# Gated linear attention and a GELU feed-forward: two stages with a DRAM bridge, rewritten as one software pipeline over 512-token groups

## The chip, the cores and the metric

The kernel runs on one core of a Trainium2 chip. The metric is the device time of one execution in microseconds (us). A core has a matrix engine (PE, whose weight loads are listed apart as PEld), a vector engine (DVE), an activation engine (ACT), a general engine (POOL) and SP, which here issues DMAs.

## The reference

```python
f = 1.0 / (1.0 + np.exp(-f_logit))
state = np.zeros((B, H, D, D), dtype=np.float32)
for t in range(S):
    state = f[:, :, t, :, None] * state + np.einsum('bhd,bhe->bhde', k[:, :, t], v[:, :, t])
    y[:, :, t] = np.einsum('bhd,bhde->bhe', q[:, :, t], state)
x = np.ascontiguousarray(y.transpose(0, 2, 1, 3)).reshape(B * S, H * D)
h = x @ w_in
out = (0.5 * h * (1.0 + erf(h / sqrt(2)))) @ w_out
```

B is 4, H is 8, S is 768, D is 48: 3072 tokens of 384 features. The hidden width d_ff is 2048. Inputs and output are float32.

## The kernel before

The recurrence is computed in chunks of 128 tokens, nC = 6 chunks for each of the 32 pairs (b, h). The decay becomes a running sum of log f, taken with a triangular matrix on PE (line 80), so that Q is scaled by exp of the sum and K by its reciprocal (lines 84 to 92). Per chunk, PE transposes both to 48x128 (lines 101, 103), makes the 128x128 scores AT (line 109), which ACT copies and POOL masks (lines 110, 111), and the chunk's contribution to the 48x48 state (line 116), which DVE scales and accumulates (lines 117 to 128). Two matmuls then make the output, transposed, in YT (lines 134, 135). DVE copies it and SP stores it to a DRAM tensor, `xT_bridge` (lines 137, 138).

When the attention pools are closed, the second stage loads the weights through SP, casts them on DVE (lines 150 to 156), and takes 512 tokens at a time: three matmuls into a bank `hps` for each of 16 slices of d_ff (line 172), a gelu on ACT (line 175), and four matmuls into four banks `opsum` (line 177), which DVE copies out and SP stores (lines 181, 182). There are four hps banks and four opsum banks.

The Tile framework orders the instructions of each engine by its own scheduler: it moves pieces of neighbouring (b, h) past each other. Each engine takes its own in order, and waits on semaphores. SP's queue holds the loads, the bridge's 192 stores, and only then the two weight loads and the loads of line 167.

Of the kernel before, what the change touches and what calls it, by code (L numbers as in the profile page):

```python
# [8 lines left out]
F32 = mybir.dt.float32  # L9
AF = mybir.ActivationFunctionType  # L10
ALU = mybir.AluOpType


@with_exitstack
def kernel(
# [10 lines left out]
    nc = tc.nc  # L26
    B, H, S, D = q.shape
    C = 128
    nC = S // C
    d_model = moe_w_in.shape[0]  # L30
    d_ff = moe_w_in.shape[1]
    n_tok = B * S
    assert d_model == H * D

    BF16 = mybir.dt.bfloat16
    xT = nc.dram_tensor("xT_bridge", (d_model, n_tok), BF16, kind="Internal").ap()

    singles = ctx.enter_context(tc.tile_pool(name="singles", bufs=1))
    tri = singles.tile([C, C], BF16)
    nc.gpsimd.memset(tri, 0.0)  # L40
    nc.gpsimd.affine_select(
        out=tri, in_=tri, compare_op=ALU.is_gt, fill=1.0,
        base=0, pattern=[[-1, C]], channel_multiplier=1,
    )
    ident = singles.tile([C, C], BF16)
    make_identity(nc, ident)
    ones_col = singles.tile([C, 1], BF16)
    nc.gpsimd.memset(ones_col, 1.0)

    attn_ctx = ExitStack()  # L50
    sb = attn_ctx.enter_context(tc.tile_pool(name="sb", bufs=4))
    ps = attn_ctx.enter_context(tc.tile_pool(name="ps", bufs=1, space=bass.MemoryType.PSUM))
    s0_pool = attn_ctx.enter_context(tc.tile_pool(name="s0", bufs=4))

    q_r = q.rearrange("b h (c t) d -> b h t c d", t=C)
    k_r = k.rearrange("b h (c t) d -> b h t c d", t=C)
    v_r = v.rearrange("b h (c t) d -> b h t c d", t=C)
    f_r = f_logit.rearrange("b h (c t) d -> b h t c d", t=C)

    for b in range(B):  # L60
        for h in range(H):
            fl = sb.tile([C, nC, D], F32)
            nc.sync.dma_start(out=fl, in_=f_r[b, h])
            q_td = sb.tile([C, nC, D], F32)
            nc.sync.dma_start(out=q_td, in_=q_r[b, h])
            k_td = sb.tile([C, nC, D], F32)
            nc.sync.dma_start(out=k_td, in_=k_r[b, h])
            vv_f = sb.tile([C, nC, D], F32)
            nc.sync.dma_start(out=vv_f, in_=v_r[b, h])
            vv_all = sb.tile([C, nC, D], BF16)  # L70
            nc.vector.tensor_copy(vv_all, vv_f)

            sig = sb.tile([C, nC, D], F32)
            nc.scalar.activation(sig, fl, AF.Sigmoid)  # L74
            lf = sb.tile([C, nC, D], BF16)
            nc.scalar.activation(lf, sig, AF.Ln)  # L76

            gln = ps.tile([C, nC, D], F32)
            glast_p = ps.tile([D, nC], F32)
            nc.tensor.matmul(gln.rearrange("c n d -> c (n d)"), tri, lf.rearrange("c n d -> c (n d)"), start=True, stop=True)  # L80
# [38 lines left out]
            S_all = sb.tile([D, nC, D], BF16)  # L119
# [93 lines left out]
```

## Time and profile before

| | |
|---|---|
| runs | 514.59, 513.13, 513.49 us; median 513.49 |
| profiled execution | span 513.5 us, first to last instruction; 7385 instructions |
| PE busy | 371.6 us, 72% |
| ACT busy | 342.9 us, 67% |
| DVE busy | 256.6 us, 50% |
| POOL busy | 65.0 us, 13% |
| granted clock of PE, mean | 0.994 of full speed |
| DMA | 35.10 MB, 68 GB/s over the span |

The profile lists how long each engine was at work, what each group of instructions cost (line, tile written and tile read, shapes, count, busy time, mean), and what ended the idle time before it (the releaser). The chain of waits follows the last instruction back from releaser to releaser. A queue is written SPq. A busy PE is not a full PE, since ends of pipelined matmuls are modelled.

### The profile page before, as it was taken

How to read it: one execution, taken by the hardware profiler on the slowest of the kernel's cores; microseconds unless marked ns; L12 is line 12 of the kernel's file. 1: busy time of each engine (PE TensorE's matmuls, PEld its weight loads, DVE VectorE, ACT ScalarE, POOL GpSimd, SP SyncE). 2: the span in 40 equal slices, each digit the busy share in tenths (PEclk: the TensorE clock that was granted, in tenths of full speed). 3: DMA queues.
4: the chain of work that ended last, by engine and by line, in shares of the span. 5: the costliest groups of instructions: out<-in, count | busy, mean ns of one | idle time of the engine just before them, and what ended most of it. 6: DMA issues, size and time to landing. Idle time of an engine off the chain costs nothing.

```text
span 513.5 us, 7385 instructions
## 1 busy us (share of the span) xinstructions
PE 371.6 (72%) x2048; PEld 183.1 (36%) x2048; DVE 256.6 (50%) x1018; ACT 342.9 (67%) x897; POOL 65.0 (13%) x201
## 2 busy tenths in 40 slices
PE   1666666655677776677877777674179899999995
PEld 0333333332333343343434443332034344444442
DVE  1777767776667567755567777863220110101001
ACT  8999999999998889978785454432034344444442
POOL 0021121111111211222221121211000000000000
PEclk9999999999999999999999999999989999999998
DMA  9544433334334224322322220002910211201011
GB/s 164 83 97 98 97 63 79 64 63 94 66 66 86 53 45 93 68 43 43 73 42 57 45 56 11 7 9 54 396 49 0 93 57 37 92 2 63 0 63 61
DMA packets 121002, 35.10 MB, mean 68 GB/s; under 512 B 113152, under 2 KB 120576, under 8 KB 120576
## 3 DMA queue, kind: packets, MB, share of 16 engines
q1 hardware_dynamic: 120960, 34.63, 29.4%
q8 instruction: 16, 0.26, 0.2%
q14 instruction: 26, 0.21, 0.1%
HBM read 27.53 MB, written 7.08 MB: 67 GB/s over the span
## 4 chain that ended last, share of the span: by engine, by line
PE 46%; ACT 34%; issue 8%; DMA 6%; DVE 6%; POOL 0%; SPq 0%; ACTq 0%; DVEq 0%
PE opsum L177 13%; PE hps L172 11%; PE AT L109 6%; ACT L76 5%; ACT L74 5%; PE YT L135 5%; ACT KpT L106 4%; ACT ATm_all L110 4%; PE KpTp L103 4%; DMA wout_f<-in_moe_w_out_dram 4%; ACT L84 4%; PE YT L134 3%; ACT QpT_all L104 3%; PE QpTp L101 2%; ACT lf L76 2%
## 5 line engine op out<-in xcount | busy, mean ns | idle before, releaser
L175 ACT ACTIVATE gT<-hps 128x512 bf16<-128x512 f32 x96 | 57.2, 597 | 77.2 <-PE hps L172 61.0
L111 POOL TENSOR_SCALAR_AFFINE_SELECT ATm_all<-ATm_all 128x128 bf16<-128x128 bf16 x192 | 63.9, 333 | 286.2 <-ACT ATm_all L110 286.1
L137 DVE CAST YTs<-YT 48x128 bf16<-48x128 f32 x192 | 52.4, 273 | 70.2 <-PE YT L135 68.5
L109 PE MATMUL AT<-QpT_all,KpT 48*128 48x128 bf16 x192 | 54.7, 285 | 45.0 <-ACT KpT L106 44.0
L172 PE MATMUL hps<-xTt,win_sb 128*128 128x512 bf16 x288 | 73.3, 387 | 16.0 <-DVE win_sb L152 16.0
L177 PE MATMUL opsum<-wout_sb,gT 128*128 128x384 bf16 x384 | 75.0, 333 | 5.0 <-DVE wout_sb L156 2.8
L181 DVE COPY osb<-opsum 128x384 f32<-128x384 f32 x24 | 12.3, 552 | 119.2 <-PE opsum L177 109.2
L134 PE MATMUL YT<-ATm_all,vv_all 128*48 128x128 bf16 x192 | 58.4, 304 | 18.0 <-DVE YTs L137 15.1
L110 ACT ACTIVATE ATm_all<-AT 128x128 bf16<-128x128 f32 x192 | 51.8, 270 | 27.9 <-PE AT L109 27.9
L104 ACT ACTIVATE QpT_all<-QpTp 48x128 bf16<-48x128 bf16 x192 | 50.2, 261 | 20.9 <-PE QpTp L101 19.4
L117 DVE TENSOR_SCALAR Scon_all<-Scontrib,Glast_all 48x48 f32<-48x48 f32 x192 | 48.6, 253 | 30.2 <-PE Scontrib L116 26.5
L88 DVE RECIPROCAL rGT_all<-GT_all 128x288 f32<-128x288 f32 x32 | 61.9, 1935 | 1.5 <-ACT GT_all L84 1.5
L101 PE MATMUL QpTp<-ident,Qp_all 128*48 128x128 bf16 x192 | 58.1, 303 | 5.4 <-ACT QpT_all L104 3.2
L116 PE MATMUL Scontrib<-vv_all,Kp_all 128*48 128x48 bf16 x192 | 44.0, 229 | 20.7 <-DVE Scon_all L117 18.2
L103 PE MATMUL KpTp<-ident,Kp_all 128*48 128x128 bf16 x192 | 57.8, 301 | 0.1
L135 PE MATMUL YT<-QpT_all,S_all 48*48 48x128 bf16 x192 | 57.4, 299 | 0.0
L106 ACT ACTIVATE KpT<-KpTp 48x128 bf16<-48x128 bf16 x192 | 50.8, 264 | 4.7 <-PE KpTp L103 3.0
L109 PEld LDWEIGHTS <-KpT 48*128 48x128 bf16 x192 | 19.4, 101 | 88.8 <-ACT KpT L106 78.6
L177 PEld LDWEIGHTS <-gT 128*128 128x128 bf16 x384 | 31.3, 99 | 47.8 <-ACT gT L175 27.4
L172 PEld LDWEIGHTS <-win_sb 128*128 128x128 bf16 x288 | 28.5, 99 | 46.1 <-issue 19.3
L76 ACT ACT_TABLE_LOAD x32 | 41.1, 1283 | 0.9 <-PE glast_p L82 0.3
L74 ACT ACT_TABLE_LOAD x29 | 37.2, 1283 | 1.3 <-PEq L197 0.8
(37 smaller groups left out, 389.2 us busy)
## 6 DMA issues: line engine op xcount, KB each, us to landing
fl<-in_f_logit_dram SPq DMA_DIRECT2D x32, 144.0 KB, 2.7
q_td<-in_q_dram SPq DMA_DIRECT2D x32, 144.0 KB, 2.6
k_td<-in_k_dram SPq DMA_DIRECT2D x32, 144.0 KB, 2.6
vv_f<-in_v_dram SPq DMA_DIRECT2D x32, 144.0 KB, 2.5
out_dram<-osb SPq DMA_DIRECT2D x24, 192.0 KB, 2.0
xT_bridge<-YTs SPq DMA_DIRECT2D x192, 12.0 KB, 1.4
win_f<-in_moe_w_in_dram SPq DMA_DIRECT2D x1, 3072.0 KB, 10.0
wout_f<-in_moe_w_out_dram SPq DMA_DIRECT2D x1, 3072.0 KB, 19.2
```

What stands on the lines that cost most here:

```text
L76: nc.scalar.activation(lf, sig, AF.Ln)
L101: nc.tensor.transpose(QpTp, Qp, ident)
L103: nc.tensor.transpose(KpTp, Kp, ident)
L104: nc.scalar.activation(QpT_all[:, c, :], QpTp, AF.Copy)
L106: nc.scalar.activation(KpT, KpTp, AF.Copy)
L109: nc.tensor.matmul(AT, KpT, QpT_all[:, c, :], start=True, stop=True)
L110: nc.scalar.activation(ATm_all[:, c, :], AT, AF.Copy)
L111: nc.gpsimd.affine_select(out=ATm_all[:, c, :], in_=ATm_all[:, c, :], compare_op=ALU.is_ge, fill=0.0, base=0, pattern=[[1, C]], channel_mu ...
L134: nc.tensor.matmul(YT, vv_all[:, c, :], ATm_all[:, c, :], start=True, stop=False)
L135: nc.tensor.matmul(YT, S_all[:, c, :], QpT_all[:, c, :], start=False, stop=True)
L172: nc.tensor.matmul(hps, win_sb[:, ko, fo * 128:(fo + 1) * 128], xTt[:, ko, :], start=(ko == 0), stop=(ko == KO - 1))
L177: nc.tensor.matmul(opsum[s], gT[:, s * 128:(s + 1) * 128], wout_sb[:, fo, :], start=(fo == 0), stop=(fo == FO - 1))
```

## The change

The loops over (b, h) and the second stage go. The 24 chunks of 128 tokens, all eight heads each, are taken in six groups of four: 512 tokens, one tile of the feed-forward part.

- **Stage 1 of a group** (`stage1`): exp(-f_logit) in place, then Ln(x + 1), which is -log f; the running sum with a negated triangular matrix `trin`; gt and rg are Exp of the sum and of its negative; DVE multiplies q and k by them, POOL casts v into `vp`, a padded layout. Sixteen matmuls and an Exp give the decay over each chunk, gl.
- **Attention of a chunk** (`attn`): two heads are put side by side on the partitions (48 of 64 each). Eight transposes fill one bank `tp`; ACT copies kT, DVE makes qb (two copies into a block layout with zeros), ACT copies qT. Scores come in two halves through one bank `ap`, masked by DVE. The state is updated with DVE (the sum) and POOL (the product and the casts into `sb`). The output goes through bank `yp` straight to xT in SBUF, in a row order that w_in's rows are loaded in as well.
- **Feed-forward of a group** (`ffn_group`): f1 is 16 units of three matmuls and a gelu; f2 is, for each of four blocks of 128 tokens, four units of four matmuls into one bank `op`, which ACT copies to `osb`.
- **Order**: the schedule is the order of the code (`manual_schedule`). In round g, f1 and f2 of group g are laid between the attention units of group g+1 and the stage 1 units of group g+2.
- **Loads**: inputs are loaded by SP per chunk and tensor, 16 DMAs a group. The weights are loaded and cast to bfloat16 by 28 DMAs on POOL's queue, at the start.

The diff, cut to its core:

```diff
-    for b in range(B):
-        for h in range(H):
...
-                nc.sync.dma_start(out=xT[h * D:(h + 1) * D, b * S + t0: b * S + t0 + C], in_=YTs)
-    attn_ctx.close()
...
+    ctx.enter_context(tc.manual_schedule())
+    ld = ctx.enter_context(tc.tile_pool(name="ld", bufs=2))
+    hp = ctx.enter_context(tc.tile_pool(name="hp", bufs=3, space=PSUM))
+    pp = ctx.enter_context(tc.tile_pool(name="pp", bufs=1, space=PSUM))
...
+    def load_win():
+        for kk in range(KO):
+            for g in range(4):
+                for hh in range(2):
+                    r = (2 * kk + hh) * D + 16 * g if g < 3 else (6 + hh) * D + 16 * kk
+                    nc.gpsimd.dma_start(out=win[32 * g + 16 * hh:32 * g + 16 * hh + 16, kk, :],
+                                        in_=moe_w_in[r:r + 16, :])
...
+        def u_exp(j):
+            nc.scalar.activation(t["fl"][:, j], t["fl"][:, j], AF.Exp, scale=-1.0)
+        def u_ln(j):
+            nc.scalar.activation(lf[:, j, :, 0:D], t["fl"][:, j], AF.Ln, bias=1.0)
+        def u_g(j):
+            gps = hp.tile([C, H, D], F32, name="hps")
+            nc.tensor.matmul(gps, trin, lf[:, j, :, 0:D], start=True, stop=True)
+            nc.scalar.activation(gt, gps, AF.Exp)
+            nc.scalar.activation(rg, gps, AF.Exp, scale=-1.0)
+            nc.vector.tensor_tensor(qp[:, j, :, 0:D], t["qt"][:, j], gt, ALU.mult)
+            nc.vector.tensor_tensor(kp[:, j, :, 0:D], t["kt"][:, j], rg, ALU.mult)
...
+        def u_t():
+            tp = pp.tile([C, 2, P2, C], BF16, name="tp")
+            for i, src in enumerate((kp, qp)):
+                for p in range(P2):
+                    nc.tensor.transpose(tp[:, i, p, :], src[:, j, 2 * p:2 * p + 2, :], ident)
+            nc.scalar.activation(kT, tp[:, 0], AF.Copy)
+            nc.vector.tensor_copy(qb[0:D, :, 0, :], tp[0:D, 1])
+            nc.vector.tensor_copy(qb[64:64 + D, :, 1, :], tp[64:64 + D, 1])
+            nc.scalar.activation(qT, tp[:, 1], AF.Copy)
+        def u_a(half):
+            ap_ = pp.tile([C, 4, C], F32, name="ap")
+            for i in range(2):
+                p = 2 * half + i
+                nc.tensor.matmul(ap_[:, 2 * i:2 * i + 2, :], x["kT"][:, p, :], x["qb"][:, p],
+                                 start=True, stop=True)
+            nc.vector.tensor_tensor(x["am"][:, 4 * half:4 * half + 4, :], ap_,
+                                    mask.unsqueeze(1).to_broadcast([C, 4, C]), ALU.mult)
...
+        def f1(fo):
+            hps = hp.tile([C, TOK], F32, name="hps")
+            for kk in range(KO):
+                nc.tensor.matmul(hps, win[:, kk, fo * 128:(fo + 1) * 128], xT[:, kk, :],
+                                 start=(kk == 0), stop=(kk == KO - 1))
+            nc.scalar.activation(gT[:, fo, :], hps, AF.Gelu)
+        def f2(s, r):
+            if r == 0:
+                st["o"] = pp.tile([C, d_model], F32, name="op")
+            for fo in range(4 * r, 4 * r + 4):
+                nc.tensor.matmul(st["o"], gT[:, fo, s * C:(s + 1) * C], wout[:, fo, :],
+                                 start=(fo == 0), stop=(fo == FO - 1))
+            if r == 3:
+                nc.scalar.activation(osb, st["o"], AF.Copy)
+                nc.sync.dma_start(out=out[r0:r0 + C, :], in_=osb)
...
+    load(0)
+    load_win()
+    load(1)
+    load_wout()
+    for f in stage1(0):
+        f()
+    spread(attn_group(0), stage1(1), 0.3, 1.0)
+    for g in range(NG):
+        f1, f2 = ffn_group(g)
+        if g + 2 < NG:
+            load(g + 2)
+        att = attn_group(g + 1) if g + 1 < NG else []
+        st1 = stage1(g + 2) if g + 2 < NG else []
+        k1 = len(att) // 2
+        spread(f1, att[:k1])
...
+        spread(f2, seq, 0.0, 0.85)
```

How this moves instructions is seen on three engines. On ACT, before, in the attention stage: copies of one chunk, and table loads between them.

```order
L106 ACTIVATE KpT<-KpTp 48x128
L104 ACTIVATE QpT_all<-QpTp 48x128
L86 ACTIVATE Glast_all<-glast_p 48x6
L74 ACT_TABLE_LOAD
L74 ACTIVATE sig<-fl 128x288
L110 ACTIVATE ATm_all<-AT 128x128
L106 ACTIVATE KpT<-KpTp 48x128
L104 ACTIVATE QpT_all<-QpTp 48x128
L76 ACT_TABLE_LOAD
L76 ACTIVATE lf<-sig 128x288
```

Now, in a steady round (the kernel's lines are those of the new file: 282 gelu, 190 and 195 the copies kT and qT, 130 exp, 133 Ln, 294 osb):

```order
L282 ACTIVATE gT<-hps 128x512 x7
L190 ACTIVATE kT<-tp 128x512
L195 ACTIVATE qT<-tp 128x512
L282 ACTIVATE gT<-hps 128x512 x8
L190 ACTIVATE kT<-tp 128x512
L195 ACTIVATE qT<-tp 128x512
L130 ACT_TABLE_LOAD
L130 ACTIVATE fl<-fl 128x384 x3
L294 ACTIVATE osb<-op 128x384
L130 ACTIVATE fl<-fl 128x384
L133 ACT_TABLE_LOAD
L133 ACTIVATE lf_96<-fl 128x8x48
```

Gelus of one group and attention copies of the next now stand in one row, and the copy of an output block, osb, stands behind a table load and three exps.

On PE, before, in the attention stage: short matmuls of neighbouring chunks.

```order
L116 MATMUL Scontrib<-vv_all,Kp_all 48x48
L109 LDWEIGHTS KpT
L109 MATMUL AT<-QpT_all,KpT 128x128
L103 LDWEIGHTS Kp_all
L103 MATMUL KpTp<-ident,Kp_all 48x128
L134 LDWEIGHTS vv_all
L134 MATMUL YT<-ATm_all,vv_all 48x128
L101 LDWEIGHTS Qp_all
L101 MATMUL QpTp<-ident,Qp_all 48x128
```

Now, in the first half of a round (280 is hps, 202 the scores):

```order
L280 LDWEIGHTS win
L280 MATMUL hps<-xT,win 128x512
L280 LDWEIGHTS win
L280 MATMUL hps<-xT,win 128x512
L280 LDWEIGHTS win
L280 MATMUL hps<-xT,win 128x512
L202 LDWEIGHTS kT
L202 MATMUL ap<-qb_103,kT 128x256
L202 LDWEIGHTS kT
L202 MATMUL ap<-qb_103,kT 128x256
L280 LDWEIGHTS win
L280 MATMUL hps<-xT,win 128x512
```

Feed-forward matmuls now stand between the links of the attention chain.

On POOL, before, from its first instructions (names of the masks and of ATm_all as in the code):

```order
L40 MEMSET tri 128x128
masks.py:197 MEMSET ident 128x128
L41 ISA
L41 AFFINE_SELECT tri<-tri 128x128
masks.py:199 AFFINE_SELECT ident<-ident 128x128
L48 MEMSET ones_col 128x1
L111 AFFINE_SELECT ATm_all<-ATm_all 128x128 x192
```

Now, at the same place (104 and 110 are the weights, 148 the cast of v, 224 and 229 the state):

```order
L90 MEMSET kp_100 128x32x16
L104 DMA win<-in_moe_w_in_dram 16x2048 x24
L110 DMA wout<-in_moe_w_out_dram 128x4x384 x4
L148 CAST vp_101<-vt 128x8x3x16 x4
L229 CAST sb_106<-tn 48x4x3x16 x2
L224 TENSOR_TENSOR tn<-rr,gl 128x384
L229 CAST sb_105<-tn 48x4x3x16 x2
L224 TENSOR_TENSOR tn<-rr,gl 128x384
```

The weights' 28 DMAs have moved from SP, where they came after all of attention, to POOL, ahead of the first cast of v.

## Rows read from the trace of the kernel before

**Rows 1.** The page's part 1: busy time and share of the span, each engine.
```profile
PE 371.6 (72%) x2048; PEld 183.1 (36%) x2048; DVE 256.6 (50%) x1018; ACT 342.9 (67%) x897; POOL 65.0 (13%) x201
```

**Rows 2.** Windows by stage: stretch, its length, busy time by engine, PE's granted clock, DMA share, GB/s.
```profile
12.80:345.00 332.20, 230.43 (x1329) 119.06 (x1330) 229.46 (x958) 270.11 (x772) 62.13 (x186) 1.00 0.31 62
...
355.00:372.00 17.00, 1.95 (x5) 0.73 (x6) 3.36 (x1) 0.44 (x1) 0.00 (x0) 1.00 0.89 328
372.00:513.50 141.50, 131.06 (x668) 59.12 (x666) 15.62 (x25) 58.05 (x97) 0.00 (x0) 0.98 0.14 48
```

**Rows 3.** The page's part 4: the chain that ended last, by engine.
```profile
PE 46%; ACT 34%; issue 8%; DMA 6%; DVE 6%; POOL 0%; SPq 0%; ACTq 0%; DVEq 0%
```

**Rows 4.** The page's part 6, DMA issues: count, KB each, us to landing.
```profile
xT_bridge<-YTs SPq DMA_DIRECT2D x192, 12.0 KB, 1.4
...
wout_f<-in_moe_w_out_dram SPq DMA_DIRECT2D x1, 3072.0 KB, 19.2
```

**Rows 5.** Timeline of SP: start us, us, queue, line; the first loads and the last stores.
```profile
8.43 0.70 SPq L69 DMA_DIRECT2D vv_f<-in_v_dram  x1
...
336.13 18.61 SPq L138 DMA_DIRECT2D xT_bridge<-YTs  x14
```

**Rows 6.** Groups on ACT: line, tile, shapes, count, busy us, mean ns, idle before, releasers.
```profile
L175 ACT ACTIVATE gT<-hps 128x512 bf16<-128x512 f32 x96 | 57.2, 597 | 77.2 <-PE hps L172 61.0 <-PE opsum L177 13.9
...
L110 ACT ACTIVATE ATm_all<-AT 128x128 bf16<-128x128 f32 x192 | 51.8, 270 | 27.9 <-PE AT L109 27.9
...
L76 ACT ACT_TABLE_LOAD x32 | 41.1, 1283 | 0.9 <-PE glast_p L82 0.3
...
L76 ACT ACTIVATE lf<-sig 128x288 bf16<-128x288 f32 x32 | 14.2, 442 | 0.4
```

**Rows 7.** Chain of waits in the feed-forward stage: start us, us, what.
```profile
450.23 1.36 PE opsum L177 x8
451.59 1.29 PE hps L172 x6
```

**Rows 8.** Groups on the weight loads of PE, on DVE and on POOL.
```profile
L111 POOL TENSOR_SCALAR_AFFINE_SELECT ATm_all<-ATm_all 128x128 bf16<-128x128 bf16 x192 | 63.9, 333 | 286.2 <-ACT ATm_all L110 286.1
...
L137 DVE CAST YTs<-YT 48x128 bf16<-48x128 f32 x192 | 52.4, 273 | 70.2 <-PE YT L135 68.5
...
L177 PEld LDWEIGHTS <-gT 128*128 128x128 bf16 x384 | 31.3, 99 | 47.8 <-ACT gT L175 27.4 <-issue 6.5
...
L90 DVE TENSOR_TENSOR Qp_all<-q_td,GT_all 128x288 bf16<-128x288 f32 x32 | 14.2, 443 | 1.7 <-PE QpTp L101 1.7
...
L181 DVE COPY osb<-opsum 128x384 f32<-128x384 f32 x24 | 12.3, 552 | 119.2 <-PE opsum L177 109.2 <-DMA out_dram<-osb 10.0
```

**Rows 9.** Timeline of PE: the first decay sums, and the first feed-forward matmuls.
```profile
6.19 0.40 PE L82 MATMUL glast_p<-ones_col,lf 128*48 128x1 bf16 x6
...
370.43 6.18 PE L172 MATMUL hps<-xTt,win_sb 128*128 128x512 bf16 x20
```

**Rows 10.** Timeline of ACT around a table load, and of two neighbouring evacuations.
```profile
7.59 1.28 ACT L76 ACT_TABLE_LOAD   x1
8.88 0.44 ACT L76 ACTIVATE lf<-sig 128x288 bf16<-128x288 f32 x1
...
16.61 0.26 ACT L110 ACTIVATE ATm_all<-AT 128x128 bf16<-128x128 f32 x1
16.77 0.26 ACT L104 ACTIVATE QpT_all<-QpTp 48x128 bf16<-48x128 bf16 x1
```

**Rows 11.** Windows of 3 us: the first input loads, and the weight loads.
```profile
6.00:9.00 3.00, 0.59 (x7) 0.42 (x7) 0.31 (x1) 2.96 (x4) 0.00 (x0) 1.00 1.35 194
...
364.00:367.00 3.00, 0.00 (x0) 0.00 (x0) 0.41 (x1) 0.00 (x0) 0.00 (x0) 1.00 1.00 399
```

**Rows 12.** The end of the chain of waits.
```profile
506.61 1.00 PE opsum L177 x5
...
508.22 1.90 DMA out_dram<-osb
```

More of the change, by code (lines that the diff above doesn't have):

```diff
@@ L9, with spread @@
 F32 = mybir.dt.float32
+BF16 = mybir.dt.bfloat16
 AF = mybir.ActivationFunctionType
 ALU = mybir.AluOpType
+def spread(main, fill, lo=0.0, hi=1.0):
+    n, m, done = len(main), len(fill), 0
+    for i, f in enumerate(main):
+        f()
+        share = ((i + 1) / n - lo) / (hi - lo)
+        want = min(m, max(0, int(share * m + 0.5)))
+        while done < want:
+            fill[done]()
+            done += 1
+    while done < m:
+        fill[done]()
+        done += 1
 @with_exitstack
@@ L29 @@
     nC = S // C
+    NCH = B * nC
     d_model = moe_w_in.shape[0]
     d_ff = moe_w_in.shape[1]
[L32 to L44, printed above, removed]
@@ new lines @@
+    nc.gpsimd.memset(mask, 0.0)
+    nc.gpsimd.affine_select(out=mask, in_=mask, compare_op=ALU.is_gt, fill=1.0,
+                            base=0, pattern=[[-1, C]], channel_multiplier=1)
+    negcol = one.tile([C, 1], BF16, name="negcol")
+    nc.gpsimd.memset(negcol, -1.0)
+    lfs = [one.tile([C, GC, H, 64], BF16, name=f"lf{i}") for i in range(2)]
+    qps = [one.tile([C, GC, H, 64], BF16, name=f"qp{i}") for i in range(2)]
+    kps = [one.tile([C, GC, H, 64], BF16, name=f"kp{i}") for i in range(2)]
@@ new lines, with load_wout @@
+    win = one.tile([C, KO, d_ff], BF16, name="win")
+    wout = one.tile([C, FO, d_model], BF16, name="wout")
+    def load_win():
[5 more added lines that the diff above has]
+                                        in_=moe_w_in[r:r + 16, :])
+    def load_wout():
+        wo = moe_w_out.rearrange("(fo fi) m -> fi fo m", fi=128)
+        for j in range(4):
+            nc.gpsimd.dma_start(out=wout[:, 4 * j:4 * j + 4, :], in_=wo[:, 4 * j:4 * j + 4, :])
@@ new lines, in attn_group @@
+    def attn_group(g):
+        G[g]["xT"] = ffn.tile([C, KO, TOK], BF16, name="xT")
+        us = [attn(g * GC + j) for j in range(GC)]
+        seq = []
+        for j in range(GC):
+            a = us[j]
+            seq += [a[0], a[1], a[2], a[3], a[4]]
+        order = []
+        for j in range(GC):
+            a = us[j]
+            if j == 0:
+                order.append(a[0])
+            order += [a[1], a[3], a[2]]
+            if j + 1 < GC:
+                order.append(us[j + 1][0])
+            order.append(a[4])
+        return order
@@ new lines @@
+    load(0)
[3 more added lines that the diff above has]
+    for f in stage1(0):
+        f()
+    spread(attn_group(0), stage1(1), 0.3, 1.0)
[7 more added lines that the diff above has]
+        spread(f1, att[:k1])
+        a2, seq = att[k1:], []
+        n = max(len(a2), len(st1))
+        for i in range(n):
+            seq += st1[i:i + 1] + a2[i:i + 1]
+        spread(f2, seq, 0.0, 0.85)
```

249 lines of the change are left out of this document (130 added, 119 removed).

## The prediction

> **What bounds the kernel now.** I read the page's totals first: no engine is full, PE at 72% and ACT at 67% [rows 1]. Such an average hides the stages, so next come the windows by stage [rows 2]. They show three stretches that share almost nothing. Up to 345 us attention runs with ACT busy 270 of 332 us and PE 230, much of it waiting on short results. From 355 to 372 us nearly everything stands while weights arrive at 328 GB/s. From 372 us the feed-forward part runs: PE busy 131 of 141.5 us, ACT 58. The chain of waits over the span agrees: PE 46%, ACT 34%, DMA 6% [rows 3]. So ACT's and PE's idle halves lie at different times, and laying them on each other is where time can come from. The profiled execution's span is 513.5 us; the median of the runs is 513.49, so the sum below needs no correction.
>
> **What goes.** The 192 bridge stores, each 1.4 us to landing [rows 4], and the 17 us gap go; SP's queue ran 18.6 us for the last 14 stores [rows 5], and the weights stood behind them. Sigmoid and reciprocal go. Table loads of 1283 ns fall from 32 in one row alone [rows 6] to 22 in all, counted in the new ACT order. Per (batch, head) 128x48 pieces become four paired heads at a time: each ACT or DVE instruction covers 384 or 512 columns in place of 128, so its fixed part is paid less often.
>
> **PE per group of 512 tokens.** In the feed-forward stage the chain advances 6 hps matmuls in 1.29 us (0.215 each) and 8 opsum in 1.36 us (0.170) [rows 7]: 48 x 0.215 + 64 x 0.170 = 10.3 + 10.9 us. For 128-column attention matmuls, which each bring new weights, no row repeats the form. Below: opsum's rate per column, 0.170 x 128/384 = 0.057 us. Above: the weight load of 99 ns if nothing hides it [rows 8]. Six one-column matmuls with 48-column weights took 0.40 us [rows 9], so neither end is reached there; I take the middle, 0.08. Per chunk: 8 transposes 0.64, 4 score matmuls of 256 columns at 0.107 = 0.43, 4 state 0.32, 12 output 0.96: 2.35 us. Four chunks 9.4, four decay sums 0.7, 16 end sums 1.3. PE needs 10.3 + 10.9 + 11.4 = **32.6 us per group**. The Trainium skill, TensorE: Matmul & The Clock Gate, section Back-to-back issue gap, gives 81 ns for such a stream of weight load and matmul; by it the sum would stand, and no row here shows it.
>
> **ACT per group.** A 512-column evacuation takes 597 ns and one of 128 takes 270 ns [rows 6], so 0.85 ns a column; 384 columns from PSUM take 0.49 us, from SBUF 442 + 96 x 0.85 = 0.52. Sixteen gelus 9.6; eight copies kT, qT 4.8; exp and ln 8 x 0.52 = 4.2; gt, rg 8 x 0.49 = 3.9; four osb 2.0; gl 0.2; four table loads (Exp, Ln, Exp, Gelu) 5.1. In the new order qT also waits for DVE's two qb copies, which wait for kT; DVE's PSUM reads took 273 ns at 128 columns and 552 at 384 [rows 8], so 1.09 ns a column and 0.69 us for 512: four waits of 1.4 us, 5.6. That is 35.4 us without overlap. Two evacuations started 0.16 us apart though each took 0.26 [rows 10], so some 15 neighbours give back 0.1 each: **34 us**. Behind a waiting qT stand the gelus, and behind them PE, which has three hps banks.
> A table load ended at 8.87 us and the next activation began at 8.88 [rows 10], so I charge 1.283 us and no more. The Trainium skill, ScalarE: Activation LUTs, section What ACT_TABLE_LOAD costs, adds a drain of about 1.38 us for each switch: 22 x 1.38 = 30 us more in the sum, were it so; this trace shows none.
>
> **Others.** DVE per chunk: two 384-column products 0.55 each (443 ns at 288 columns [rows 8]), qb 1.4, two masks 1.4, state 0.55, four xT copies 0.55 + 3 x 0.27: 5.8 us, 23 per group, beside the 37.5 below. POOL: one 384-column product and three casts; affine_select took 333 ns for 128 columns [rows 8], so at most three times that each, 4 us per chunk, 16 per group, hidden. Loads: 3.15 MB per group at the 194 GB/s of the first loads [rows 11] is 16 us of each group; SP issues them ahead of the next outputs, each issue about 0.7 us [rows 5]. They cost nothing while a group lasts over 25 us.
>
> **Handoffs.** With PE at 32.6 and ACT at 34, neither can run free. There is one bank for op: s1 cannot start until osb of s0 is copied, and that copy stands on ACT behind kT, qT, a table load and three exps (0.6 + 1.4 + 0.6 + 1.3 + 1.6 = 5.5 us after f2 starts), while PE reaches it after about 4 (16 opsum 2.7, one output 0.96, half a score, one state). PE loses some 1.5 us there, 1 at s2, whose bank waits for the Ln load, kT and qT ahead of osb of s1, and 0.9 when the Gelu table loads after osb of s3; in f1 the wait for qb and for gelu costs about 1.5. PE 32.6 + 4.9 = **37.5 us per group**, between 34 (ACT's sum, all else hidden) and 42 (half of ACT's overlap lost and each handoff 1 us later).
>
> **Start.** ACT's first four exps come before any Ln, so the 13th of 16 loads gates them: 2.56 MB at 194 GB/s is 13 us plus 2.5 to the first data. The weights (6.3 MB, 16 us at the 399 GB/s of the old weight loads [rows 11]) now go at the same time through POOL's queue with a cast, and POOL casts vp, which the first state matmul needs, only after all 28 of them. POOL's issue price has no row. Below, 28 x 0.7 as on SP's queue [rows 5] put the first vp cast at 22 us; above, it stands behind all 12.6 MB, 16 + 33 us, at 52; I take 36, about the middle, for the first state matmul. The 13th load I put at 20 us and the end of the first stage 1 at 29 (9.3 us of ACT), between 16 without weights and 32 with all ahead. Alone, a chunk costs DVE's 4.7 us (without the products): 45.5 after two. Group 1's last fl is the 29th load, 5.7 MB; alone 32 us, with all weights ahead 48; I take 42. Then exp, Ln table, three ln, kT, qb, qT, ln, Exp table: 50, and the last chunk's 7.7 us on DVE with the products: 58. PE then meets a dense stream after sparse work; after the pause at 355 us the first 20 hps took 6.18 us [rows 9] where 20 x 0.215 is 4.3, so I add 2: **60 us** (50 to 75).
>
> **Sum.** Start 60; groups 0 to 3, 4 x 37.5 = 150; group 4 without stage 1: PE 30.7 + 3.3 = 34; group 5 alone: 10.3 + 10.9 + three osb handoffs of 0.8 + 0.4 = 24; tail 0.49 + 0.5 + 1.9 for the last store [rows 12] = 3. **271 us.** Ends: 50 + 4 x 34 + 31 + 23 + 3 = 243 and 75 + 4 x 42 + 38 + 26 + 3 = 310.
>
> **Rivals.** (a) *The stages do not overlap.* Every order is fixed; if each handoff is late, a group costs its feed-forward (22.9 us, a sixth of 370.4 to 507.6 [rows 9, 12]) plus its attention alone (4 x 5.8 on DVE, 12.2 of stage 1 on ACT): 58. Then 60 + 4 x 58 + 46 + 24 + 3 = 365. For it: one bank each for tp, ap, sp, yp, op, and ap is used twice per chunk. Against: two to four feed-forward units stand between links of the attention chain. 0.10.
> (b) *Handoffs hide.* ACT at 34 is the period: 243 if the start is 50 too. For it: before, PE was busy 131 of 141.5 us beside ACT with four banks [rows 2]. Against: one op bank. 0.13.
> (c) *Weights hold up the inputs.* Loads come in 192-byte pieces, weights in long ones. If weights win every turn and the cast runs at a third of the 399 GB/s, they take 48 us, the 29 loads 30 us more, and 16 + 2 follow the 29th as above: start 96, sum 307. Its chance is 0.12: the only rows with heavy traffic have one busy queue, so they speak neither way. The Trainium skill, DMA: Bandwidth & Descriptors, section Queues, rings and completion order, says that an engine takes turns between its queues packet by packet, so that long packets would get more than short ones; no run here shows it.
> (d) *Slower than before.* The cast loads trickle: 28 DMAs, eight outstanding, POOL blocked, group 0's state and all of f1 behind them. From 271 to 515 needs the start at 304 us, 10.8 us for each of the 28 one after another; the bridge's stores ran 1.33 us each so [rows 5], and a whole weight of 3 MB took 19.2 us [rows 4]. 0.03, with 0.01 for about equal.
> (e) That the change doesn't interleave is excluded by PE's order, which shows hps matmuls between score matmuls.
>
> **Numbers.** Forecast 0.61, (a) 0.10, (b) 0.13, (c) 0.12, (d) 0.04 with its neighbour. The range 243 to 315 takes the forecast's ends, most of (b) and the near part of (c); 0.18 stays out. A measurement tells 0.3%, 1.5 us, from no change: faster 0.96, same 0.01, slower 0.03.
>
> **What would show it.** Right: the first hps matmul at 50 to 70 us; six rising blocks some 37 us apart; ACT busiest, near 85%, with 22 table loads; osb the releaser of PE at s1; qT waiting for DVE. Wrong: a first hps after 80 us, with POOL's queue the releaser (c, d); groups of 55 us or more with DVE or POOL naming PE's waits (a); 34 us or less (b). The forecast fails if the group period leaves 34 to 42 us or the start 50 to 75.

## Result and profile after

The changed kernel takes **263.77 us** (median of 4 runs, 262.81 to 265.64) against 513.31 us (median of 4) for the kernel before on the same chip: ratio 0.5147, 95% interval 0.5124 to 0.5169. The forecast was 271, its range 243 to 315. The profiled execution is the slowest of the four, 265.64 us; its span, first to last instruction, is 263.9.

The page of the profiled execution after: totals, slices of 6.6 us each, the costliest groups, and the DMA issues.

```profile
span 263.9 us, 3983 instructions
...
PE 188.5 (71%) x1432; PEld 116.3 (44%) x1432; DVE 129.9 (49%) x266; ACT 160.8 (61%) x292; POOL 61.7 (23%) x125
...
PE   0001364525997887996879968879788799789984
...
ACT  2005832673677867878778787588886785209611
...
PEclk9999999975799999999999979999999999999999
DMA  8999999999400117991149920099910000010011
...
L290 PE MATMUL op<-wout,gT 128*128 128x384 bf16 x384 | 74.4, 330 | 15.1 <-ACT osb L294 15.1
L280 PE MATMUL hps<-xT,win 128*128 128x512 bf16 x288 | 72.2, 387 | 1.0 <-DVE xT L248 0.9
L282 ACT ACTIVATE gT<-hps 128x512 bf16<-128x512 f32 x96 | 54.5, 599 | 7.0 <-PE hps L280 5.0
...
L192 DVE COPY qb<-tp 48x512 bf16<-48x512 bf16 x24 | 10.0, 417 | 43.9 <-ACT kT L190 43.8
L195 ACT ACTIVATE qT<-tp 128x512 bf16<-128x512 bf16 x24 | 14.3, 598 | 23.6 <-DVE qb L193 23.6
L130 ACT ACTIVATE fl<-fl 128x384 f32<-128x384 f32 x24 | 11.6, 516 | 27.1 <-DMA fl<-in_f_logit_dram 27.1
...
fl<-in_f_logit_dram SPq DMA_DIRECT2D x24, 192.0 KB, 4.7
```

Half the PE time of before is gone with the small pieces (371.6 us [rows 1], now 188.5), yet its share is nearly the same: 72% then, 71% now, since the span fell with it. The idle time is in two places: the left quarter of the PE line, while DMA stands at 9 (the start), and a few tenths in every later slice.

The windows of the stages after (same columns as [rows 2]; the start's last part, rounds 0 to 3 cut where the Gelu table is loaded, group 4's round, group 5):

```profile
31.10:64.40 33.30, 14.38 (x120) 11.52 (x120) 21.74 (x46) 14.94 (x30) 8.70 (x16) 0.88 1.22 186
64.40:100.40 36.00, 32.21 (x239) 19.32 (x240) 21.05 (x45) 26.48 (x49) 6.67 (x12) 0.93 0.18 40
100.40:134.40 34.00, 29.30 (x241) 18.40 (x240) 20.33 (x44) 26.78 (x50) 6.40 (x13) 1.00 0.71 117
134.40:171.10 36.70, 31.09 (x242) 19.06 (x240) 21.14 (x45) 27.00 (x50) 8.19 (x15) 0.95 0.68 108
171.10:205.60 34.50, 29.26 (x238) 18.15 (x237) 21.00 (x44) 26.86 (x50) 6.67 (x12) 1.00 0.71 115
205.60:237.40 31.80, 27.80 (x219) 17.39 (x218) 16.56 (x36) 15.87 (x29) 4.54 (x9) 1.00 0.07 26
237.40:263.90 26.50, 21.21 (x112) 10.75 (x110) 0.00 (x0) 12.02 (x21) 0.00 (x0) 1.00 0.10 38
```

Four rounds at 34 to 36.7 us: PE is busy 29 to 32 us of each, ACT 27 beside it. What [rows 2] showed one after the other (ACT 270 of 332 us, then PE 131 of 141.5) now lies side by side. The two long rounds are those with a granted clock under 1.

Where PE stood in a round, from its timeline in round 2 (start, duration, what; in brackets the idle time ahead and its releaser):

```profile
137.86 0.38 PE L202 MATMUL ap<-qb,kT 128*128 128x256 bf16 x2 [1.50 <-DVE qb L193]
...
155.04 1.42 PE L290 MATMUL op<-wout,gT 128*128 128x384 bf16 x4 [2.00 <-ACT osb L294]
156.26 0.63 PE L202 MATMUL ap<-qb,kT 128*128 128x256 bf16 x2
...
161.85 1.46 PE L290 MATMUL op<-wout,gT 128*128 128x384 bf16 x8 [0.83 <-ACT osb L294]
...
166.80 0.27 PE L240 MATMUL yp<-am,vp 128*128 128x128 bf16 x2 [1.14 <-DVE am L204]
```

These are the handoffs: qb in f1, osb of s0 and s1 on ACT, and one mask. Behind the 2.00 us pause PE ran at the lower level of its clock (granted clock 0.50 from 156.2 to 158.0 us): four op matmuls took 1.42 us where four take 0.81 elsewhere.

### The profile page after: what moved, and what is told of

It reads as the page before. It is cut to its first block, busy times and chain, and to the rows that moved or that the text cites. A ratio compares the mean times of both kernels' runs of the same rounds, so it can differ in the third digit from the quotient of the medians.

```text
span 263.9 us, 3983 instructions
## 1 busy us (share of the span) xinstructions
PE 188.5 (71%) x1432; PEld 116.3 (44%) x1432; DVE 129.9 (49%) x266; ACT 160.8 (61%) x292; POOL 61.7 (23%) x125
## 5 line engine op out<-in xcount | busy, mean ns | idle before, releaser
L290 PE MATMUL op<-wout,gT 128*128 128x384 bf16 x384 | 74.4, 330 | 15.1 <-ACT osb L294 15.1
L280 PE MATMUL hps<-xT,win 128*128 128x512 bf16 x288 | 72.2, 387 | 1.0 <-DVE xT L248 0.9
L204 DVE TENSOR_TENSOR am<-ap,mask 128x512 bf16<-128x512 f32 x48 | 33.2, 691 | 27.7 <-PE ap L202 27.2
L280 PEld LDWEIGHTS <-win 128*128 128x128 bf16 x288 | 27.7, 99 | 26.6 <-issue 3.2
L224 POOL TENSOR_TENSOR tn<-rr,gl 128x384 f32<-128x384 f32 x16 | 13.5, 842 | 107.7 <-DVE rr L223 85.0
L202 PE MATMUL ap<-qb,kT 128*128 128x256 bf16 x96 | 20.2, 296 | 22.1 <-DVE qb L193 15.4
L192 DVE COPY qb<-tp 48x512 bf16<-48x512 bf16 x24 | 10.0, 417 | 43.9 <-ACT kT L190 43.8
L229 POOL CAST sb<-tn 48x192 bf16<-48x192 f32 x40 | 15.3, 382 | 44.8 <-DVE tn L220 42.8
L294 ACT ACTIVATE osb<-op 128x384 f32<-128x384 f32 x24 | 11.7, 488 | 22.1 <-PE op L290 18.7
L240 PE MATMUL yp<-am,vp 128*128 128x128 bf16 x192 | 20.7, 234 | 6.0 <-DVE am L204 6.0
L202 PEld LDWEIGHTS <-kT 128*128 128x128 bf16 x96 | 9.4, 102 | 32.6 <-issue 21.6
L240 PEld LDWEIGHTS <-vp 128*128 128x128 bf16 x192 | 16.9, 106 | 10.0 <-issue 6.8
L248 DVE CAST xT<-yp 32x128 bf16<-32x128 f32 x72 | 20.6, 286 | 1.2
L243 PE MATMUL yp<-qT,sb 128*128 128x128 bf16 x80 | 16.2, 233 | 0.0
```

The lines of the kernel that those rows point to most:

```text
L202: nc.tensor.matmul(ap_[:, 2 * i:2 * i + 2, :], x["kT"][:, p, :], x["qb"][:, p], start=True, stop=True)
L204: nc.vector.tensor_tensor(x["am"][:, 4 * half:4 * half + 4, :], ap_, mask.unsqueeze(1).to_broadcast([C, 4, C]), ALU.mult)
L229: nc.gpsimd.tensor_copy(dst[:, :, :, 16 * hh:16 * hh + 16], tn[64 * hh:64 * hh + D, :, D * hh:D * hh + D] .rearrange("q p (g y) -> q p g y ...
L240: nc.tensor.matmul(yp[:, p, :], vwin(vp, j, h), x["am"][:, h, :], start=(hh == 0), stop=(hh == 1 and c == 0))
L243: nc.tensor.matmul(yp[:, p, :], sb[:, p, :], x["qT"][:, p, :], start=False, stop=True)
L248: nc.vector.tensor_copy(xT[96:128, kk, j * C:(j + 1) * C], yp[32 * kk:32 * kk + 32, 3, :])
```

## Experiments

**What the overlap is worth.** The attention and stage 1 units of a round are put ahead of its feed-forward, nothing else changes.

```diff
-        spread(f1, att[:k1])
+        for f in att:
+            f()
+        for f in st1:
+            f()
+        for f in f1 + f2:
+            f()
+        continue
```

> Nothing is interleaved in the rounds: attention of the next group, then stage 1, then the feed-forward matmuls. The price of the interleaving, and rival (a) of the prediction. T: a round is 23 us of feed-forward, four chunks of about 6 us, 12 of stage 1, less 3 that the engines overlap by themselves: 56; 64 + 4 x 56 + 46 + 26 = 360 us (335 to 385). R (PE's stream sets the time in either order): below 300.

Measured: 342.36 us (2 runs, 341.01 to 343.71; ratio 0.667). A round lasts some 51 us (Gelu table loads at 91.36, 142.22, 193.85 and 244.65), 15 to 16 more on average than before this edit; five rounds of that are the 78.6 us of difference. Interleaving is worth about 79 of the 250 us gained. The larger part, about 171 us, comes with the other changes together: the wider pieces (ACT was busy 342.9 us in 897 instructions before [rows 1], now 160.8 us in 292), the missing bridge, the weights loaded at the start. No run parts these from each other.

**Is it ACT that holds osb?** The copy of op is put on DVE.

```diff
-                nc.scalar.activation(osb, st["o"], AF.Copy)
+                nc.vector.tensor_copy(osb, st["o"])
```

> Theory T (PE's own stream is about 29 us per group of the changed kernel; the rest of the 34 us period is PE waiting for the one op bank, whose copy stands on ACT behind kT, qT, a table load and three exps; the start is set by the shared DMA queues): with the copy on DVE, PE's waits of 1.7 us at s1 and 0.95 at s2 go in five rounds, 10 to 13 us in all; 252 us (248 to 256), and no PE wait named after osb above 0.8 us. Rival R (the period is PE's own stream and its clock, ACT only follows): 262 to 266, and PE's idle time turns up elsewhere. Rival D (DVE is as crowded as ACT in f2, 13 of 18 us): the copy stands behind products on DVE instead, 260 to 270.

Measured: 266.0 us (265.49 to 266.98; 0.5178 [0.5159, 0.5196]), not quicker, against T and within the ranges of both rivals; the waits below speak for D. PE's waits for osb are not shorter on the other engine:

```profile
PE op L290 <- DVE osb L294: 17.8, 18, 1.6
```

It was 15.1 us on ACT. DVE's queue at those places is as full as ACT's: in round 0's second half DVE was busy 13.1 us of 18.0 here, ACT 13.5 of 17.4 in the changed kernel. The longest of the waits, 1.60 us, ends with an osb copy at 90.55 that stood behind two qb and four xT copies.

**A second op bank**, taken from the three hps banks.

```diff
-    hp = ctx.enter_context(tc.tile_pool(name="hp", bufs=3, space=PSUM))
+    hp = ctx.enter_context(tc.tile_pool(name="hp", bufs=2, space=PSUM))
+    op = ctx.enter_context(tc.tile_pool(name="op", bufs=2, space=PSUM))
...
-                st["o"] = pp.tile([C, d_model], F32, name="op")
+                st["o"] = op.tile([C, d_model], F32, name="op")
```

> Two banks for op, and two instead of three for hps. T: PE no longer waits for osb at s1, s2 (1.7 and 0.95 us a round), 10 us in five rounds and 2 in the last group; with two hps banks f1 stops behind each pair kT, qT (about 2 us of ACT) for some 0.5 to 1 us, three per round: 257 us (252 to 264). R (osb is not what PE lacks): only the loss, 266 to 280.

Measured: 269.24 us (268.26 to 271.54; 0.5262), slower, and out of T's range. The osb waits are gone from PE's list, and others stand in their place:

```profile
PE ap L203 <- DVE qb L194: 17.4, 12, 4.0
PE hps L281 <- ACT gT L283: 10.1, 13, 1.0
PE yp L241 <- DVE am L205: 9.0, 5, 2.0
```

Two hps banks don't carry PE over a kT copy and a gelu; the third bank is worth more there than a second op.

**qT ahead of qb.** qT no longer stands on ACT behind DVE's two copies.

```diff
             nc.scalar.activation(kT, tp[:, 0], AF.Copy)
+            qT = at.tile([C, P2, C], BF16, name="qT")
+            nc.scalar.activation(qT, tp[:, 1], AF.Copy)
             qb = qbs[n % 2]
...
-            qT = at.tile([C, P2, C], BF16, name="qT")
-            nc.scalar.activation(qT, tp[:, 1], AF.Copy)
```

> qT is copied straight after kT, before DVE's two copies of the same bank, so ACT no longer waits 0.94 us for DVE 24 times (23.6 us in the changed kernel). T: only two of the four waits of a round stand ahead of an osb copy that PE waits for, so some 1 to 1.5 us per round, five rounds: 258 us (255 to 261); scores come 0.5 us later. R: 262 to 266. If ACT's sum were the period, all four waits would come off: 34 - 3.8, 264 - 19 = 245.

Measured: 260.91 us (260.43 to 261.65; 0.5083): some 3 us. All four waits of qT are gone, and yet the total is far from the 245 that would have come if ACT's sum were the period. The osb waits fell from 15.1 to 5.5 us, the qb waits rose from 15.4 to 19.6. The place is the first chunk of a round; PE's timeline there, with this edit:

```profile
97.67 1.46 PE L280 MATMUL hps<-xT,win 128*128 128x512 bf16 x6
101.12 0.38 PE L202 MATMUL ap<-qb,kT 128*128 128x256 bf16 x2 [1.99 <-DVE qb L195]
...
102.15 2.30 PE L280 MATMUL hps<-xT,win 128*128 128x512 bf16 x5
```

The transposes come only after the Gelu table has been asked for, so kT, qT and qb stand behind a table load and a gelu, and then the clock drops too (5 matmuls in 2.30 us).

**The next group's first transposes, kT and qT at the end of f2**, ahead of the Gelu table, on top of the last edit.

```diff
+    att = attn_group(1)
+    att.pop(0)()
     for g in range(NG):
...
-        att = attn_group(g + 1) if g + 1 < NG else []
...
-        k1 = len(att) // 2
+        k1 = (len(att) - 1) // 2
...
+        att = attn_group(g + 2) if g + 2 < NG else []
+        if att:
+            seq.append(att.pop(0))
         spread(f2, seq, 0.0, 0.85)
```

> On top of e2 (qT straight after kT): the transposes of the next group's first chunk, and so kT and qT, come at the end of f2, before the Gelu table is loaded, in place of after the first f1 unit. In e2's second round PE still lost 2.0 us waiting for qb behind that load and the first gelu, and its clock fell to 0.95. Theory S (PE's own stream is 29 us of the 34 to 34.5; the rest are several waits in a row, each of which shows when the one before it is taken away): this wait goes, rounds of 32 to 33 us, 253 us (250 to 257). Theory A (some one engine's sum, ACT's at 27 us plus its waits, holds the period at 34): no change, 259 to 263.

Theory S held. Measured: 252.48 us (250.17 to 252.97; 0.4913 [0.4887, 0.4939]). In the profiled execution, the quickest of the four (250.17), all four rounds stand at 32 us and at full clock (the other three took 252.2 to 253.0 at a mean granted clock of 1.00 against its 0.97, so that mean does not rank the times); two of the rounds:

```profile
64.70:97.00 32.30, 29.43 (x237) 17.93 (x236) 21.00 (x44) 27.56 (x50) 6.67 (x12) 1.00 0.22 43
97.00:128.90 31.90, 29.69 (x241) 18.17 (x240) 20.32 (x45) 27.59 (x50) 6.39 (x13) 1.00 0.68 125
```

PE is busy 29.4 to 29.7 of it: the handoffs have shrunk from some 5 us a round to under 3, and PE is what is left.

**The start: f_logit first.** A group's loads come by kind, f_logit ahead of q, k and v.

```diff
-            for n, src in (("fl", f_logit), ("qt", q), ("kt", k), ("vt", v)):
...
+        for j in range(GC):
+            one_load("fl", f_logit, j)
+        for j in range(GC):
+            for n, src in (("qt", q), ("kt", k), ("vt", v)):
+                one_load(n, src, j)
```

> The four loads of f_logit of a group come first, ahead of q, k and v. T (the 13th and 29th load gate the start): group 0's last exp moves from 23 us to about 9, group 1's from 49.5 to about 40; stage 1 of group 0 then waits for kt of the last chunk as before (15th load), so the gain is the wait of the last two chunks of group 0: first hps at 54 to 58 us in place of 64.4, 256 us (253 to 259). Rival C (the chain of copies, masks and outputs of group 0, one chunk after another, sets the start): first hps at 62 to 65, 261 to 265.

Measured: 255.77 us (254.91 to 255.94; 0.4978), the first feed-forward matmul at 57.38 in place of 64.45. Between the two profiled executions the start gave 7.1 us; rounds 1 and 3 are the old ones, round 0 was 0.9 us shorter, and round 2 was 1.7 shorter with its clock at 1.00. ACT's timeline, and below it two lines of DVE's, show where the gain ended:

```profile
16.89 0.60 ACT L194 ACTIVATE kT<-tp 128x512 bf16<-128x512 bf16 x1
28.97 0.60 ACT L199 ACTIVATE qT<-tp 128x512 bf16<-128x512 bf16 x1 [11.48 <-DVE qb L197]
...
37.92 0.52 ACT L134 ACTIVATE fl<-fl 128x384 f32<-128x384 f32 x1 [3.88 <-DMA fl<-in_f_logit_dram]
```

```profile
19.67 0.56 DVE L146 TENSOR_TENSOR qp<-qt,gt 128x384 bf16<-128x384 f32 x1 [3.26 <-DMA qt<-in_q_dram]
...
25.98 0.83 DVE L146 TENSOR_TENSOR qp<-qt,gt 128x384 bf16<-128x384 f32 x1 [3.90 <-DMA qt<-in_q_dram]
```

Stage 1's ACT part ended at 17 instead of 31, and then ACT stood 11 us for qb: DVE's products of the last two chunks waited for their q and k, 9.1 us in four pieces, and qb was queued behind them.

**The start: w_out later**, in the middle of group 0's attention.

```diff
-    load_wout()
...
-    spread(attn_group(0), stage1(1), 0.3, 1.0)
+    first = attn_group(0)
+    spread(first[:10] + [load_wout] + first[10:], stage1(1), 0.3, 1.0)
```

> The four DMAs of w_out (3.1 MB read) are issued in the middle of group 0's attention in place of ahead of POOL's first cast. In the changed kernel the first four loads of group 1 took 14 us on SP's queue while w_out moved, later ones about 1 us each. T (queues share the engines; group 1's last fl gates the start): group 1's loads come 8 us earlier, first hps at 56 to 59 us, 257 us (254 to 261); w_out then slows loads of group 2, which nobody awaits. Rival C (group 0's own chain sets the start): first hps at 62 to 65, 261 to 265.

Measured: 260.26 us (259.78 to 260.58; 0.5072), the first feed-forward matmul at 61.49, 3 us sooner. In SP's queue the loads no longer wait; of the changed kernel:

```profile
24.77 3.93 SPq L120 DMA_DIRECT2D qt<-in_q_dram  x1
28.74 4.28 SPq L120 DMA_DIRECT2D kt<-in_k_dram  x1
33.07 3.51 SPq L120 DMA_DIRECT2D vt<-in_v_dram  x1
36.62 0.79 SPq L120 DMA_DIRECT2D fl<-in_f_logit_dram  x1
```

and with w_out later:

```profile
26.29 0.90 SPq L120 DMA_DIRECT2D qt<-in_q_dram  x1
27.24 0.98 SPq L120 DMA_DIRECT2D kt<-in_k_dram  x1
28.27 0.94 SPq L120 DMA_DIRECT2D vt<-in_v_dram  x1
```

The inputs came far sooner, but of their gain only 3 us arrive. From 32 us to the first feed-forward matmul neither ACT nor DVE waits for a load any more: what is left is group 0's own chain, some 7 us a chunk.

**Both, and the rounds' edits.** On top of the version of 252.48 us: loads by kind (f_logit, then q and k, then v), w_in in thirds and w_out in halves between group 0's attention units.

```diff
+        for names in (("fl",), ("qt", "kt"), ("vt",)):
...
     load(0)
-    load_win()
+    load_win(0)
     load(1)
-    load_wout()
...
+    a = attn_group(0)
+    late = [lambda: load_win(1), lambda: load_win(2), lambda: load_wout(0), lambda: load_wout(1)]
+    for i, at_ in enumerate((4, 8, 13, 16)):
+        a.insert(at_ + i, late[i])
+    spread(a, stage1(1), 0.3, 1.0)
```

> On top of e7: f_logit first, then q and k, then v in each group's loads; one third of w_in ahead of POOL's first cast, the rest and w_out between units of group 0's attention. e4 took 7 us off the start, e5 3, where the chain of group 0's four chunks then decided (7 us a chunk). T: inputs of group 0 and 1 no longer stand behind weights, group 0's scores start at about 20 us in place of 33, and four chunks of 7 us follow: first hps at 47 to 52 us, 12 to 16 us less than e7: 240 us (235 to 246). If the weights now come too late for the first hps: 250 to 260, with POOL's queue as PE's releaser.

Measured: 234.79 us (234.50 to 235.68; 0.4580 [0.4564, 0.4595]), just under the expected 235 to 246. The first feed-forward matmul is at 48.12:

```profile
48.12 1.47 PE L282 MATMUL hps<-xT,win 128*128 128x512 bf16 x3 [3.31 <-DVE xT L250]
```

What PE waits for there is a load. DVE's xT copies stand behind a product of the next group, which waited for k:

```profile
46.65 0.56 DVE L145 TENSOR_TENSOR kp<-kt,rg 128x384 bf16<-128x384 f32 x1 [3.12 <-DMA kt<-in_k_dram]
```

That load was issued at 35.27, took 4.02 us of SP's queue and landed 11.3 us after its issue, beside the first half of w_out (issued at 36.16): the weights still seem to hold inputs here, which no run tests.

**What the clock costs.** Three feed-forward matmuls take 0.81 us at full clock (133.81 in the changed kernel's trace, for one); the first three here took 1.47. The price was measured first on the changed kernel: 8 unread 384-column matmuls after each attention unit of group 0.

```diff
+    def warm():
+        for _ in range(8):
+            nc.tensor.matmul(dm.rearrange("p (a c) -> p a c", c=C), ident,
+                             mask.unsqueeze(1).to_broadcast([C, 3, C]), start=True, stop=True)
...
+    for u in attn_group(0):
+        a += [u, warm]
+    spread(a, stage1(1), 0.3, 1.0)
```

> The changed kernel with 8 matmuls of 384 columns, whose result nobody reads, after each attention unit of group 0: only PE's clock in the first round is at stake. In the changed kernel the clock was 0.88 from 31 to 64 us and 0.86 from 64 to 83, and that round took 36.7 us where the second took 34.0. Clock theory: the first round takes 34 to 34.5 us with the clock at 1.00; the start is 0 to 3 us longer; 262 to 264. If the first round is long for another reason (loads of the next group, cold caches): it stays at 36 to 37, and the total is 264 to 268.

Measured: 266.89 us (266.24 to 267.31; 0.5199), clock 1.000 over the whole profiled execution. The rounds (from one Gelu table load to the next) are 35.5, 34.0, 35.0 and 34.5 us against 36.7, 34.0, 36.7 and 34.5: 1.2 and 1.7 us less, so the low clock cost 2.9 us in the changed kernel's trace. Counted from its first feed-forward matmul, round 0 fell from 36.0 to 34.5. But the first Gelu table came at 68.41 instead of 63.79: the unread matmuls stood in group 0's chain and cost 4.6, where at most 3 was expected, and the total missed the clock theory's 262 to 264.

The 1.7 us of round 2 are not the unread matmuls' doing. With f_logit first and with w_out later, which have none, that round took 35.0 us at a clock of 1.00 as well. The pause ahead of s1 is there each time; with f_logit first, and here:

```profile
147.06 0.81 PE L294 MATMUL op<-wout,gT 128*128 128x384 bf16 x4 [1.99 <-ACT osb L298]
...
158.41 0.81 PE L290 MATMUL op<-wout,gT 128*128 128x384 bf16 x4 [2.00 <-ACT osb L294]
```

So the length of this pause does not settle whether the clock falls behind it; what does stays open.

Then on the version of 234.79 us, only in the last part of the start: 8 and 10. The 8 were meant for the wait behind the last chunk's first score half; the edit puts them earlier, behind the last chunk's transposes and ahead of the third chunk's output matmuls.

```diff
+    a.insert(15, lambda: fill(8))
...
     att.pop(0)()
+    fill(10)
```

> The quickest version so far (inputs by kind, weights spread, next group's transposes early: 234.79 us) plus unread 384-column matmuls that PE can run where it stands in the last part of the start: 8 after the last chunk's first score half, where it waited 3.40 us for the mask, and 10 right before the first feed-forward matmul, where it waited 3.31 us for xT. In that version the granted clock was 0.79 at 30 to 46 us, 0.50 at 46 to 52 and 0.92 at 52 to 58, and the first 21 feed-forward matmuls with the attention between them took 8.1 us where the same stream at clock 1.00 takes about 5.6. Theory K (the low clock of the first round is what the pauses of the start leave behind, and costs some 2.5 us): 232.3 us (231.5 to 233.3), clock 1.00 from the first feed-forward matmul on, the first one no later than 48.5 us. Rival N (these matmuls' time is hidden behind ACT, or the fill delays the last chunk as much as it gives back): 234.3 to 236.5 us.

Measured: 236.28 us (235.85 to 237.21; 0.4617 [0.4602, 0.4631]): no gain, the total that N gave. The first 24 feed-forward matmuls, with the attention between them, went through in 6.56 us (50.47 to 57.03) instead of 8.7 (48.12 to 56.83), as was hoped, but began 2.35 us later, so that K's price is about right and the fill took it back. The 8 held up the third chunk's output and what follows from it; the next transposes came at 46.47 in place of 43.79, and the 10 behind them ran until 50.47, though xT was ready at 47.72.

Last, only the 10 that fill the wait for xT.

> The version with inputs by kind, spread weights and early transposes (234.79 us) plus only the 10 unread matmuls right before the first feed-forward matmul, where PE waited 3.31 us for xT; the 8 in the last chunk, which in the run before stood ahead of the third chunk's output matmuls and moved the first feed-forward matmul from 48.12 to 50.47, are left out. Ten such matmuls took 3.41 us at the low clock, so they just fill the wait. Theory K (the low clock after the pause costs about 2.3 us, as 6.56 against 8.9 us for the first 24 feed-forward matmuls showed, and PE's time is what counts there): first feed-forward matmul at 48.2 to 48.6, 232.0 to 233.5 us. Rival N (the next limit, ACT or the qb wait, takes what the clock gives back, or the clock stays low since it was 0.50 and 0.79 before): 234 to 235.5 us, the next group's table loads at the same times as without the fill.

Measured: **233.16 us** (232.99 to 234.2; 0.4555 [0.4541, 0.4569]), in K's range and the quickest of all, though its interval just meets that of the version without them. In PE's timeline:

```profile
44.39 2.79 PE L312 MATMUL op<-mask,ident 128*128 128x384 bf16 x10
47.19 1.29 PE L282 MATMUL hps<-xT,win 128*128 128x512 bf16 x3
```

The clock at 46 to 52 us was 0.97 (0.50 without), and the next Gelu table loads at 80.00 in place of 82.52, 2.5 us sooner. Of that 0.9 is an earlier first matmul, which these matmuls don't make: the k load that DVE waits for landed at about 45.6 in place of 46.6 (issued at 33.88, 11.7 us to landing), and DVE's product of it began at 45.73 in place of 46.65. About 1.6 is the clock's: the first 24 feed-forward matmuls went through in 7.13 us instead of 8.71.

## Why the prediction was right, by its own steps

The case that was forecast came: the stages overlap, ACT and PE share the round, ACT's osb copy holds the one op bank, qT waits for DVE, the weights do not hold the start past 75 us. The sum, term by term:

| term | forecast | measured | from |
|---|---|---|---|
| start | 60 | 64.4 | first hps matmul at 64.45 |
| groups 0 to 3 | 4 x 37.5 = 150 | 141.8 | 36.7 + 34.0 + 36.7 + 34.5, between Gelu table loads at 63.79 and 205.63 |
| group 4 | 34 | 31.7 | 205.63 to 237.37 |
| group 5 and tail | 27 | 26.5 | 237.37 to the end |

The sum was 7 us too high: the start ran 4.4 us longer than forecast, the groups 11 us shorter, so part of the agreement is two errors against each other. The rounds lay at the low end of the forecast's 34 to 42, where rival (b) begins. One sign of being right did not come: ACT was to be the busiest, near 85%; it was busy 61%, PE 71%. And the prediction took the span for the time of a run, since before's span and median agreed at 513.5; here the span is 1.7 us below its own run's time (263.9 and 265.64), and these 1.7 us are in no term.

**PE per group was priced at 32.6 us; its parts add up to 28.7.** The term that was mis-sized is the 128-column attention matmul with new weights, 0.08 us between bounds 0.057 and 0.099. Twelve output matmuls take 0.67 us, 74.38 to 75.05:

```profile
74.38 0.27 PE L240 MATMUL yp<-am,vp 128*128 128x128 bf16 x2
...
75.05 1.46 PE L280 MATMUL hps<-xT,win 128*128 128x512 bf16 x6
```

That is 0.056 each: the lower end, the rate per column with the weight load of about 100 ns fully hidden. The Trainium skill, TensorE: Matmul & The Clock Gate, section Back-to-back issue gap, gives 81 ns for such a stream; the measured 56 decides, and the middle that agreed with that figure was the wrong choice. So a chunk takes 0.44 (8 transposes) + 0.43 (scores) + 0.17 (state) + 0.67 = 1.71 us instead of 2.35, four take 6.8, and the sums of stage 1 add 0.65 + 0.4 (0.7 + 1.3). The feed-forward parts were right: 48 hps in 10.36 us (10.3) and 16 op in 2.62, 10.5 a group (10.9).

**Handoffs were priced at 4.9 us; 34.0 - 28.7 is 5.3**, of which the waits that PE's timeline names make 4.7 in round 1. Single ones over the rounds: osb of s0 1.72 to 2.00 (1.5 forecast), the next 0.83 to 0.95 (1), qb in f1 1.50 (1.5). The fourth is not the Gelu table (0.9 forecast) but a mask, 0.65 to 1.14 us at yp.

**ACT per group was priced at 34 us; it is about 30.6.** Its busy time is 26.8, and the four waits of qT for qb came to 3.8 (0.94 each), not 5.6: DVE's copy of 512 bfloat16 columns on 48 partitions took 417 ns (L192 on the page above), where the f32 rows of before, 552 ns at 384 columns [rows 8], had given 0.69 us. Neighbouring activations also overlapped more than the 1.5 us allowed: gt and rg begin 0.37 us apart and last 0.5. The table loads came as charged, 22 of 1.28 us, the next activation right behind where nothing else was waited for (load at 23.56, Ln at 24.86), and Ln and Exp each asking for one of their own, as counted. Rival (b) set ACT's sum as the period; the two 34s agree by chance, since taking all of qT's waits away gave 3 us in all, and PE with its handoffs makes the measured one.

**The clock** was a term only once, +2 at the first feed-forward matmuls. It was low in rounds 0 and 2, and with full clock these lasted 2.9 us less; the four rounds are then 34.0 to 35.5 us.

**Start.** Its steps ran later than forecast, and one was shorter. The fourth exp, which waits for the 13th load, came at 23.0 (20), stage 1 ended at 31.1 (29), and group 1's last fl at 49.5 (42); from there it took 15.0 us to the first matmul (16, and 2 more for a slow stream behind it, which in the measurement falls into round 0). From ACT's timeline:

```profile
14.96 0.52 ACT L130 ACTIVATE fl<-fl 128x384 f32<-128x384 f32 x1 [6.52 <-DMA fl<-in_f_logit_dram]
23.02 0.52 ACT L130 ACTIVATE fl<-fl 128x384 f32<-128x384 f32 x1 [7.53 <-DMA fl<-in_f_logit_dram]
...
49.49 0.53 ACT L130 ACTIVATE fl<-fl 128x384 f32<-128x384 f32 x1 [1.60 <-DMA fl<-in_f_logit_dram]
```

The step that was off is when group 1's last fl lands: 7.5 us late, since SP needed 14 us for four loads (22.67 to 36.6) while w_out moved. This is rival (c) in small: the inputs did lose to the weights, for 14 us and not for 30. The Trainium skill, DMA: Bandwidth & Descriptors, section Queues, rings and completion order, has an engine take turns between its queues packet by packet, so that long packets get more than short ones. These rows agree in that the short pieces of the inputs lose beside the weights: with w_out moved, three of the four loads took some 1 us each. They do not show that length is what decides, since w_in, in rows of 2048 elements, slowed the loads less (1.6 to 2.3 us each) than w_out in rows of 384. POOL's vp cast, for which 36 us was taken, gated nothing: POOL had issued all 28 DMAs by 24.5 us (497 ns for one of w_in, 771 for w_out), and three casts were done at 26.

Rival (a) is excluded by the rounds; how far it was off is told by the run without interleaving, whose round was 51 us where 58 was worked out, so that this rival's 365 would have been about 342. Rival (d) needed 10.8 us a weight DMA; SP's loads ran at 1 us again from 36.6 us on, which suggests that the weights were through by about then.

## What to carry to other kernels

Count first what the rewrite takes off each engine: here fewer and wider instructions, with the bridge gone, came with two thirds of the gain, the overlap with one. When two stages with different limiting engines are laid on each other, the round is the busier engine's stream plus the handoffs through its single banks; count those handoffs one by one in the new order, and remove them by moving the next group's first link ahead of the table load, not by moving the copy to another engine. With the steady part at its limit, look at the start: order loads by the kind that the first step of all chunks needs, and start weights no sooner than their first use asks. For a price with a wide bound, run the cheap form of it first, or take the bound whose mechanism (a weight load hidden behind the matmul before it) the rows already show.

## What was not expected of the hardware

- **The clock after short pauses.** Behind a pause of 2.00 us at 155.04 PE ran at the lower of its two levels (1.2 GHz) until about 158.5, but behind one of 1.72 at 86.10 four op matmuls took 0.81 us, the pace at 2.4 GHz. Three pauses of 0.63 us in group 5 left the clock at 1.00. And the same 2.00 us pause in three other versions (f_logit first, w_out later, unread matmuls in the start) left it at 1.00 too.
- **Two queues at once.** A 192 KB input load took about 1.0 us of SP's queue by itself, 1.6 to 2.3 while w_in moved, and 3.5 to 4.3 while w_out moved, though w_out's rows (384 elements) are shorter than w_in's (2048).
